# The last half chunk of an FFN, packed into two column tiles and zero-padded, with the value weights loaded between token blocks and a new task order

## The chip, the cores and the metric

The kernel runs on one core of a Trainium2 chip. The metric is device time in microseconds (us) of one execution. TensorE (PE) does matmuls, ScalarE (ACT) activations, VectorE (DVE) elementwise work and statistics, GpSimd (POOL) masks and small things, SyncE (SP) issues DMAs. A run lists its mean granted TensorE clock.

## The reference

One transformer layer on 2048 tokens, width 640, in bf16: layer norm, an attention with 32 heads of 20 in four segments of 512 tokens (causal softmax inside a segment, a running linear memory of the segments before), the output projection and a residual; then layer norm, an FFN of width 1728 with SiLU, and a residual.

```python
x = A_x
h = x + _A_ref(_layernorm(x, axis=-1), A_wq, A_wk, A_wv, A_wo, A_beta)
h2 = h + _B_ref(_layernorm(h, axis=-1), B_w1, B_w2)   # silu(x @ w1) @ w2
```

The point: 1728 = 13 x 128 + 64. Of the 14 chunks of the FFN's inner width the last is half a chunk, 64 rows.

## The kernel before

The program is a list of named tasks (`h1_2_13_0`: first FFN matmul, segment 2, chunk 13; `v00`: value projection, block 0; `qk..`: scores; `e..`: their exponentials; `pr..`: q and k projections; `fill39`: 39 dummy matmuls, "fillers", that keep PE busy where it would wait). A fixed string `ORDER` says in which order tasks are issued, on which engine and in which buffer. Each engine runs its own tasks strictly in that order. The parts that matter:

```python
for f in range(NF):                                   # 14 chunks
    fw = 128 if f < NF - 1 else FF - 128 * (NF - 1)   # the last: 64
    ...
    fns = [lambda e, c=c: e.matmul(bank(ps)[0:fw, lo:hi], lhsT=w1_sb[:, c, 128 * f:128 * f + fw],
                                   rhs=hT[:, c, lo:hi], start=(c == 0), stop=(c == NC - 1)) for c in range(NC)]
    # then th = tanh(0.5 * ps) on ACT, sT = (th + 1) * ps on DVE, both on fw partitions
...
for f in range(f0, f1):                               # h2, per token block i
    fw = 128 if f < NF - 1 else FF - 128 * (NF - 1)
    for hh in range(2):
        e.matmul(bank(ps, hh)[:, 0:320], lhsT=sT[0:fw, f, 128 * i:128 * i + 128],
                 rhs=w2_sb[0:fw, f, 320 * hh:320 * hh + 320], start=(f == 0), stop=(f == NF - 1))
```

At the start the four x blocks are loaded on SP's queue. wq, wk, wv follow on ACT's queue, after a warm-up activation. `SPLIT0 = (0, 1)` cuts the projections of the first two chunks into token halves, so that they can start on blocks 0 and 1.

The softmax here doesn't subtract the row's maximum and nothing guards it: scores larger than these inputs give would overflow.

## Time and profile before

| | before |
|---|---|
| time, median of 3 | 315.74 us |
| span in the profile | 313.7 us |
| PE busy | 301.0 us (96%) |
| tile configuration changes on PE, from the matmul records | 244 |

The page's table of busy time and the clock row of its 40 slices, kernel before:

```profile
span 313.7 us, 7314 instructions
...
PE 301.0 (96%) x2918; PEld 168.7 (54%) x2918; DVE 219.0 (70%) x495; ACT 227.3 (72%) x320; POOL 142.6 (45%) x280
...
PEclk9999799999999999999999999999999999999999
```

PE is busy nearly always, so one has to ask what it is busy with. The fifth slice of the clock row (31 to 39 us) shows a 7: there the granted clock was half for 3.4 us.

The stretch view of the kernel before (columns: stretch, its length, busy us of each engine with instruction counts, granted clock, DMA share, GB/s):

```profile
0.00:18.00 18.00, 15.55 (x131) 11.98 (x131) 11.76 (x40) 7.75 (x16) 6.24 (x28) 1.00 0.76 231
18.00:60.00 42.00, 39.33 (x449) 20.37 (x441) 30.79 (x86) 37.10 (x55) 21.92 (x47) 0.96 0.61 147
60.00:100.00 40.00, 38.56 (x439) 23.05 (x432) 30.81 (x79) 37.40 (x57) 24.48 (x53) 1.00 0.47 90
...
262.00:314.00 52.00, 48.01 (x300) 27.89 (x298) 24.14 (x42) 7.96 (x14) 3.13 (x8) 1.00 0.19 50
```

The fourth busy column is ACT: 37 of 42 and 37 of 40 us early on, 8 of 52 at the end. So PE and ACT together set the pace during the attention, and PE alone at the end.

Groups by shape, kernel before (count, busy us, mean ns of one):

```profile
L1162 PE MATMUL ps_all<-w_sb,sT 64*128 64x320 bf16 x32 | 7.1, 301 | 0.0
L1130 PE MATMUL ps_all<-hT,w_sb 128*64 128x512 bf16 x15 | 3.8, 384 | 0.0
L1144 DVE SCALAR_TENSOR_TENSOR sT<-th,ps_all 64x512 bf16<-64x512 f32 x3 | 2.0, 671 | 0.0
L1138 ACT ACTIVATE th<-ps_all 64x512 f32<-64x512 f32 x3 | 1.8, 587 | 0.3 <-DVE sT L1144 0.3
```

The half chunk on 64 partitions takes as long as a whole one on 128 (the whole ones take 679 and 608 ns on DVE and ACT). And there is a cost that no mean shows. The timeline of the kernel before, inside the last h2 matmuls:

```profile
303.13 0.11 PEld L1162 LDWEIGHTS ps_all<-w_sb,sT 64*128 64x128 bf16 x2 [0.26 <-issue]
303.50 1.47 PEld L1162 LDWEIGHTS ps_all<-w_sb,sT 128*128 128x128 bf16 x12 [0.26 <-issue]
```

The weight loader, which otherwise runs ahead during the matmuls, stands still for 0.26 us before and after the 64-row weights. The starts of the single matmuls in the trace say what that costs:

```
128-row to 128-row   136 ns from start to start
128-row to  64-row   231 ns
 64-row to  64-row   146 ns
 64-row to 128-row   228 ns
```

Elsewhere in the same trace matmuls of 512 columns start 216 ns apart: 192 columns more take 80 ns, so PE streams 2.4 columns per ns, and 320 columns are 133 ns. So the visit of two matmuls costs about 0.2 us more than two more full-height matmuls would, and there are 16 visits. The Trainium skill says, in "TensorEngine Tiling (Array Packing)", section Key Properties, that changing the tiling mode drains TensorE. The trace agrees and gives the price of this change: about 95 ns on the way in and 92 on the way out, and about 10 ns on the matmul after the first.

The first loads and the first score exponentials, kernel before: the page's DMA issues (KB each, us from issue to landing), then the timeline.

```profile
sT<-in_A_wq_dram ACTq DMA_DIRECT2D x1, 800.0 KB, 7.0
sT<-in_A_wk_dram ACTq DMA_DIRECT2D x1, 800.0 KB, 8.8
wv_sb<-in_A_wv_dram ACTq DMA_DIRECT2D x1, 800.0 KB, 10.2
```
```profile
18.25 1.51 ACT L888 ACTIVATE PTE<-ps_all 128x768 bf16<-128x768 f32 x2 [0.23 <-PE ps_all L877]
```

In the trace they land at 10.1, 12.4 and 14.4 us.

### The profile page before, as it was taken

What the parts mean: (1) busy time and instruction counts of PE and PEld (TensorE: products, weight loads), DVE (VectorE), ACT (ScalarE), POOL (GpSimd) and SP (SyncE); (2) the same over time, 40 slices, a digit from 0 to 9 for tenths busy, and PEclk for the clock granted to TensorE, in tenths of its full rate; (3) what the DMA queues carried; (4) which work ended last, traced back from release to release, by engine and by line L of the source; (5) the groups of instructions that cost most, each with busy time, mean ns of one, the idle gap of its engine ahead of it and who ended that gap; (6) DMA issues with size and microseconds to landing.
All of it is one profiled execution on the core that took longest, in us unless ns stands there. A gap on an engine that the chain in (4) does not pass through costs nothing.

```text
span 313.7 us, 7314 instructions
## 1 busy us (share of the span) xinstructions
PE 301.0 (96%) x2918; PEld 168.7 (54%) x2918; DVE 219.0 (70%) x495; ACT 227.3 (72%) x320; POOL 142.6 (45%) x280
## 2 busy tenths in 40 slices
PE   8899799999999999999999999999999999999995
PEld 6655454447555445575544544546554466744563
DVE  4888567787678876785979967569865594844622
ACT  3399798999989999988899898795889940004500
POOL 5227736344497465644748454536566540300000
PEclk9999799999999999999999999999999999999999
DMA  6884546951165300045442400223440006220002
GB/s 180 273 284 103 98 110 216 168 112 28 36 99 88 76 17 3 3 82 125 81 127 19 82 4 0 44 42 72 94 101 1 2 0 107 42 65 21 0 24 104
DMA packets 48353, 24.56 MB, mean 78 GB/s; under 512 B 38848, under 2 KB 47232, under 8 KB 48320
## 3 DMA queue, kind: packets, MB, share of 16 engines
q1 hardware_dynamic: 46352, 21.65, 31.4%
q10 hardware_dynamic: 1968, 2.46, 2.5%
q8 instruction: 23, 0.38, 0.5%
q14 instruction: 10, 0.08, 0.1%
HBM read 10.33 MB, written 2.62 MB: 41 GB/s over the span
## 4 chain that ended last, share of the span: by engine, by line
PE 69%; ACT 19%; DVE 5%; issue 2%; POOL 2%; DMA 1%; ACTq 0%; DVEq 0%
PE ps_all L1162 17%; PE ps_all L1130 13%; PE ps_all L805 11%; PE ps_all L1106 7%; PE ps_all L877 6%; PE ps_all L771 5%; ACT PTA L888 5%; PE ps_all L923 5%; ACT PTB L888 4%; ACT PTE L888 4%; ACT th L1138 3%; PE ps_all L597 2%; DVE on L989 2%; PE ps_all L952 1%; DMA oT<-otok 1%
## 5 line engine op out<-in xcount | busy, mean ns | idle before, releaser
L888 ACT ACTIVATE PTA<-ps_all 128x1024 bf16<-128x1024 f32 x64 | 62.5, 1025 | 7.4 <-PE ps_all L877 6.8
L1162 PE MATMUL ps_all<-w_sb,sT 128*128 128x320 bf16 (+1 forms) x448 | 67.7, 300 | 0.0
L1130 PE MATMUL ps_all<-hT,w_sb 128*128 128x512 bf16 (+3 forms) x350 | 67.1, 337 | 0.6 <-issue 0.5
L888 ACT ACTIVATE PTB<-ps_all 128x1024 bf16<-128x1024 f32 (+1 forms) x64 | 58.8, 969 | 7.8 <-PE ps_all L877 6.9
L900 POOL TENSOR_SCALAR_AFFINE_SELECT PTB<-PTB 128x512 bf16<-128x512 bf16 x64 | 41.3, 645 | 47.4 <-ACT PTB L888 45.1
L1138 ACT ACTIVATE th<-ps_all 128x512 f32<-128x512 f32 (+3 forms) x70 | 34.6, 519 | 34.8 <-PE ps_all L1130 30.4
L1144 DVE SCALAR_TENSOR_TENSOR sT<-th,ps_all 128x512 bf16<-128x512 f32 (+3 forms) x70 | 38.7, 574 | 20.7 <-ACT th L1138 20.3
L1162 PEld LDWEIGHTS ps_all<-w_sb,sT 128*128 128x128 bf16 (+1 forms) x448 | 40.5, 97 | 22.4 <-issue 7.9
L1130 PEld LDWEIGHTS ps_all<-hT,w_sb 128*128 128x128 bf16 (+1 forms) x350 | 32.0, 99 | 28.4 <-issue 4.8
L888 ACT ACTIVATE PTE<-ps_all 128x1024 bf16<-128x1024 f32 (+1 forms) x40 | 35.6, 937 | 4.2 <-PE ps_all L877 4.0
L900 POOL TENSOR_SCALAR_AFFINE_SELECT PTE<-PTE 128x512 bf16<-128x512 bf16 x40 | 25.8, 646 | 14.7 <-ACT PTE L888 13.3
L703 DVE BATCH_NORM_STATS2 stt<-x_tok 128x6 f32<-128x320 bf16 x64 | 28.0, 479 | 2.8 <-DMA x_tok<-in_A_x_dram 2.5
L771 PE MATMUL ps_all<-wv_sb,xT 128*128 128x320 bf16 x160 | 25.8, 311 | 1.3 <-ACT PTE L888 1.3
L805 PE MATMUL ps_all<-xT,wqr 128*128 128x512 bf16 (+1 forms) x110 | 24.9, 360 | 1.6 <-DVE wqr L677 1.3
L997 POOL TENSOR_TENSOR otok<-on 128x320 bf16<-128x320 bf16 x24 | 19.1, 800 | 14.6 <-DVE on L989 14.6
L814 DVE CAST QK<-ps_all 128x512 bf16<-128x512 f32 (+1 forms) x34 | 21.0, 628 | 6.4 <-PE ps_all L805 5.7
L1172 DVE SCALAR_TENSOR_TENSOR x_tok<-ps_all,x_tok 128x640 bf16<-128x640 f32 x16 | 12.9, 819 | 17.2 <-PE ps_all L1162 17.2
L805 PE MATMUL ps_all<-xT,wkr 128*128 128x512 bf16 (+1 forms) x110 | 24.8, 361 | 0.0
L1106 PE MATMUL ps_all<-wo_sb,oT 128*128 128x320 bf16 x160 | 23.8, 299 | 0.7 <-DMA oT<-otok 0.5
L712 POOL TENSOR_TENSOR rst<-mvt,eps_c 128x1 f32<-128x1 f32 x32 | 6.9, 216 | 35.2 <-DVE mvt L706 32.3
L877 PE MATMUL ps_all<-QK 20*128 20x256 bf16 (+3 forms) x360 | 20.7, 288 | 1.5 <-ACT PTA L888 0.6
L771 PEld LDWEIGHTS ps_all<-wv_sb,xT 128*128 128x128 bf16 x160 | 15.2, 101 | 9.7 <-DMA xT<-xn_rot 1.5
(77 smaller groups left out, 409.9 us busy)
## 6 DMA issues: line engine op xcount, KB each, us to landing
out_dram<-x_tok SPq DMA_DIRECT2D x16, 160.0 KB, 2.0
w_sb<-in_B_w_dram SPq DMA_DIRECT2D x5, 432.0 KB, 6.3
x_tok<-in_A_x_dram SPq DMA_DIRECT2D x3, 640.0 KB, 5.8
w_sb<-in_B_w_dram SPq DMA_DIRECT2D x3, 480.0 KB, 4.2
QKV<-QK SPq DMA_DIRECT2D x16, 72.0 KB
sT<-in_A_wq_dram ACTq DMA_DIRECT2D x1, 800.0 KB, 7.0
sT<-in_A_wk_dram ACTq DMA_DIRECT2D x1, 800.0 KB, 8.8
wv_sb<-in_A_wv_dram ACTq DMA_DIRECT2D x1, 800.0 KB, 10.2
```

The costliest lines, as they stand in the source:

```text
L703: T.add(DV, lambda e, hh=hh: e.bn_stats(out=stt[:, s, 6 * hh:6 * hh + 6], in_=xb[:, 320 * hh:320 * hh + 320]), reads=R((xa, xsub)), writes ...
L771: fns.append(lambda e, c=c, hh=hh: e.matmul(bank(ps, hh)[:, 0:320], lhsT=xT[:, c, 128 * i:128 * i + 128], rhs=wv_sb[:, c, 320 * hh:320 * h ...
L805: fns = [lambda e, kc=kc: e.matmul(bank(ps)[:, lo:hi], lhsT=wt[:, kc, c, :], rhs=xT[:, kc, lo:hi], start=(kc == 0), stop=(kc == NC - 1)) f ...
L814: (lambda e: e.tensor_copy(out=o, in_=i_))
L877: fns.append(lambda e, j=j, o=o, r=r, q0=q0, q1=q1, qa=qa, ka=ka: e.matmul(ps_all[:, o:o + q1 - q0], lhsT=ka[32 * r:32 * r + DH, 128 * j:1 ...
L888: T.add(AC, lambda e: e.activation(out=pt[:, pta.slot, q0:q0 + 2, 0:width], in_=sc3[:, b0:b0 + 2, 0:width], func=ACT.Exp, scale=SCALE), re ...
L900: fns.append(lambda e, v=v: e.affine_select(out=v, in_=v, pattern=[[0, 4], [1, 128]], compare_op=ALU.is_ge, fill=0.0, base=0, channel_mult ...
L1106: fns.append(lambda e, c=c, hh=hh: e.matmul(bank(ps, hh)[:, 0:320], lhsT=oT[:, c, 128 * i:128 * i + 128], rhs=wo_sb[:, c, 320 * hh:320 * h ...
L1130: fns = [lambda e, c=c: e.matmul(bank(ps)[0:fw, lo:hi], lhsT=w1_sb[:, c, 128 * f:128 * f + fw], rhs=hT[:, c, lo:hi], start=(c == 0), stop= ...
L1138: T.add(AC, lambda e: e.activation(out=th[0:fw, tha.slot, lo:hi], in_=bank(ps)[0:fw, lo:hi], func=ACT.Tanh, scale=0.5), reads=R((ps, [0])) ...
L1144: T.add(DV, lambda e: e.scalar_tensor_tensor(out=sT[0:fw, f, lo:hi], in0=th[0:fw, tha.slot, lo:hi], scalar=1.0, in1=bank(ps)[0:fw, lo:hi], ...
L1162: fns.append(lambda e, f=f, fw=fw, hh=hh: e.matmul(bank(ps, hh)[:, 0:320], lhsT=sT[0:fw, f, 128 * i:128 * i + 128], rhs=w2_sb[0:fw, f, 320 ...
```

## The change

Four things at once:

1. h1 of the half chunk becomes two column tiles: the even token blocks go to output partitions 0 to 63, the odd ones to 64 to 127, side by side. Tanh and multiply then run on 128 partitions and half as many columns.
2. h2 reads that packed tile at full height. Its weights exist twice, once with rows 64 to 127 zero (even blocks), once with rows 0 to 63 zero (odd blocks). The zeros come from the warm-up activation, which is now a tanh of 0.
3. All first loads are in SP's queue, in the order x0, x1, wv, x2, x3, beta, wq, wk, without waiting for the warm-up. The value matmuls of blocks 0 and 1 come first in PE's order.
4. `SPLIT0` is empty, and the whole `ORDER` is new, with 41 fillers instead of 64.

```diff
-SPLIT0 = (0, 1)
+SPLIT0 = ()
 ORDER = """   # (all lines replaced)
-zpad:0 x0:0 x1:1 x2:2 warm x3:3 ... w_q:0 w_k beta ... w_wv:0 n1_ap0:0 fill39:0 n1_tp0:0 ...
+zpad:0 x0:0 x1:1 w_wv:0 x2:2 x3:3 beta w_q:0 w_k ... fill21:0 n1_tp0:0 ... n1_te1/A v00:0 v01:2 ...
-    for b in range(4):
-        load_x(b, 1, -100 + b, (2.2, 3.0, 3.7, 4.2)[b], "fix", (SP,))
+    load_x(0, 1, -100, 2.30, "fix", (SP,))
+    load_x(1, 1, -99, 2.33, "fix", (SP,))
+    load_w("wv", wv_sb[:, :, :], cw(A_wv), -98, 4.96, [(W["wv"], [0])], "fix", (SP,))
     ...
+    tail = f == NF - 1
+    if tail:
+        hv = hT[:, :, :].rearrange("p c (i h t) -> p c h i t", h=2, t=128)
+        fns = [lambda e, c=c, k=k: e.matmul(
+            bank(ps)[64 * k:64 * k + 64, lo:hi], lhsT=w1_sb[:, c, 128 * f:FF],
+            rhs=hv[:, c, k, b0 // 2:b1 // 2, :], start=(c == 0), stop=(c == NC - 1),
+            tile_position=(0, 64 * k)) for c in range(NC) for k in range(2)]
     ...
-    fw = 128 if f < NF - 1 else FF - 128 * (NF - 1)
+    t0, fr = (128 * i, f) if f < NF - 1 else (128 * (i // 2), f + i % 2)
     for hh in range(2):
-        ... lhsT=sT[0:fw, f, 128 * i:128 * i + 128], rhs=w2_sb[0:fw, f, 320 * hh:320 * hh + 320] ...
+        ... lhsT=sT[:, f, t0:t0 + 128], rhs=w2_sb[:, fr, 320 * hh:320 * hh + 320] ...
```

## The prediction

> **What bounds the kernel now.** The page's table of busy time has TensorE (PE) busy 301.0 of 313.7 us. By the starts of single matmuls in the trace, streaming is 261 us, 6.8 of it filler matmuls; 244 changes of tile configuration at about 0.095 us are 23 us; some 25 us are stalls, more than half before 60 us. In the stretch view ScalarE is the second limit: busy 37.1 of 42 us between 18 and 60 us, 37.4 of 40 to 100, and only 8.0 of 52 after 262 us, where PE alone sets the pace.
>
> **What the change removes and adds.**
>
> 1. Half chunk in h2. Equal matmuls start 136 ns apart; into the 64-row weights it is 231 ns, then 146, and out again 228. So each of 16 visits costs about 0.2 us. The Trainium skill ("TensorEngine Tiling (Array Packing)", Key Properties) says that changing the mode drains TensorE; the trace agrees. Zero-padded to 128 rows the matmul takes the same 133 ns and no switch. Counted in the two orders, changes fall from 244 to 217: 27 x 0.095 = 2.6 us, plus 0.3 for slower first ones.
>
> 2. Half chunk in h1. Today 5 matmuls of 512 columns at 216 ns per segment (segment 0: twice 256). As two column tiles, 5 pairs of 256 columns at about 112 ns: the packed value matmuls (L923) already start 2 to 5 ns apart, as the skill's "TensorE: Matmul & The Clock Gate", Part 3, says. 4 x 0.52 = 2.1 us of PE. Tanh and multiply on the half chunk go from 587 and 671 ns to about 390 and 417 in three segments, and from two pairs to one in segment 0: about 1 us each on ScalarE and VectorE.
>
> 3. Start. wq, wk, wv land at 10.1, 12.4, 14.4 us; ScalarE's warm-up holds their issue until 3.15 us, and between 4.4 and 6 us DMA moves about 130 KB per us against 370 later. With one queue I estimate wv at 6, wq at 9, wk at 11.3 us. Two blocks' value matmuls then replace fillers (64 become 41), and the first score exponential starts at about 15.5 us instead of 18.25. Gain 1.5 to 2.7 us for PE and ScalarE alike.
>
> 4. Unsplit projections save a few evictions. The task order is all new: about 2 us either way, unknown.
>
> **On the critical path.** After 262 us all PE savings count: two segments' h2 (1.7) and one h1 (0.5), 2.2 us. Before, ScalarE and PE alternate: the start's gain plus part of the other 2.8 us of PE, 3 to 5 us. Together about 6.3 us: 315.7 becomes 309.4 us, range 306.0 to 312.8. On the 2% line: faster 0.5, within 2% 0.48, slower 0.02.
>
> **What would show it.** h2 matmuls evenly 136 ns apart through each block; about 217 changes; half-chunk h1 pairs 2 to 5 ns apart, a group about 0.6 us; wv landed near 6 us, first score exponential near 15.5 us; the last stretch (last segment's h1 to last h2 matmul) shorter by about 1.3 us.
>
> **What would make it wrong.** wk landing later than 12.4 us (the start then gains nothing); the column tiles' weight loads (109 ns each) not hiding behind 107 ns of streaming; a longer clock drop (today half clock from 36 to 39 us) with fewer fillers; or the new order adding stalls between 20 and 160 us that eat the savings.

## More of the kernel before

In the first 18 us ACT has done only 7.75 us of work.

## The result, and the profile after

| | before | after |
|---|---|---|
| median of the same rounds | 315.62 us (4 runs) | 306.18 us (4 runs) |
| ratio | | 0.9711, 95% interval 0.9678 to 0.9744 |
| the same, second measurement | 314.82 us (11 runs) | 305.99 us (6 runs), 0.9725 (0.9698 to 0.9752) |
| span in the profile | 313.7 us | 303.9 us |
| configuration changes on PE | 244 | 217 |

A ratio is the mean time of one kernel's fast runs over the mean of the other's fast runs of the same rounds, so it is not quite the ratio of the medians. The change is faster by 2.8 to 2.9%, some 9 us; 6.3 us were predicted, and the time lies near the lower end of the range.

The same lines of the page after:

```profile
span 303.9 us, 7238 instructions
...
PE 290.1 (95%) x2876; PEld 165.8 (55%) x2900; DVE 219.1 (72%) x489; ACT 226.8 (75%) x322; POOL 143.9 (47%) x280
...
PEclk9999999999999999999999999999999999999999
```

PE is busy 10.9 us less, ACT and DVE as long as before, and the half-clock stretch is gone. Some records of matmuls are missing after (2876 matmuls beside 2900 weight loads), so sums over matmuls are short by up to a per cent, while starts and spans are not.

The stretch view after:

```profile
0.00:18.00 18.00, 15.15 (x99) 8.97 (x101) 11.48 (x34) 10.20 (x20) 6.04 (x25) 1.00 0.65 208
18.00:60.00 42.00, 38.79 (x475) 19.70 (x477) 35.63 (x98) 38.83 (x56) 24.71 (x50) 1.00 0.70 173
60.00:100.00 40.00, 39.16 (x456) 23.72 (x456) 31.85 (x77) 38.40 (x57) 24.75 (x57) 1.00 0.36 77
```

By 18 us ACT has done 10.20 us instead of 7.75, and it stays busier until 100 us. PE's busy time in the first stretch is a little lower, but fewer of its matmuls are fillers: useful streaming by 18 us, added up from the columns of each record, is 8.2 us instead of 6.8.

Groups by shape after, the answer to the four lines of before:

```profile
L1176 PE MATMUL ps_all<-w_sb,sT 128*128 128x320 bf16 x448 | 65.2, 299 | 0.0
L1138 PE MATMUL ps_all<-hT,w_sb 128*64 128x256 bf16 x30 | 2.2, 277 | 0.0
L1158 DVE SCALAR_TENSOR_TENSOR sT<-th,ps_all 128x256 bf16<-128x256 f32 x29 | 11.7, 416 | 9.1 <-ACT th L1152 8.8
L1152 ACT ACTIVATE th<-ps_all 128x256 f32<-128x256 f32 x29 | 10.8, 391 | 5.0 <-PE ps_all L1138 4.6
```

There are no 64-row matmuls any more, and the half chunk's tanh and multiply take 391 and 416 ns (three of the 29 in each group are half chunks; segment 0 has two more, of 128 columns, at 282 and 284 ns). The timeline of one packed h1 group after:

```profile
288.51 0.47 PEld L1138 LDWEIGHTS ps_all<-hT,w_sb 128*64 128x64 bf16 x10 [0.26 <-issue]
288.52 0.74 PE L1138 MATMUL ps_all<-hT,w_sb 128*64 128x256 bf16 x10
```

Single starts inside this group are 3, 130, 3, 106, 4, 105, 4, 106, 3 ns apart: the two tiles of a pair start together, and a pair follows a pair after 109 ns, about the 107 ns that 256 columns take. Five of the old 512-column matmuls were 216 ns apart. The weight loads, of 109 ns in the mean, hide. That is what the Trainium skill says of packed tiles ("TensorE: Matmul & The Clock Gate", Part 3: about 4 ns from one tile to the next).

The loads after (page, DMA issues) and the first score exponentials (timeline):

```profile
wv_sb<-in_A_wv_dram SPq DMA_DIRECT2D x1, 800.0 KB, 5.6
sT<-in_A_wq_dram SPq DMA_DIRECT2D x1, 800.0 KB, 7.8
sT<-in_A_wk_dram SPq DMA_DIRECT2D x1, 800.0 KB, 9.6
```
```profile
17.12 1.50 ACT L891 ACTIVATE PTE<-ps_all 128x768 bf16<-128x768 f32 x2
```

In the trace wv, wq, wk land at 7.4, 11.6 and 13.8 us (6.8, 11.0, 13.2 in a second profile). wk, which gates the first scores, comes later than before, not earlier. The first exponential still starts 1.1 us earlier (1.7 in the second profile). One profile's first exponential is a weak measure, though: e1 and e2 below, which keep the old start, have it at 17.6 and 17.1 us. By the 17th the two orders are well apart: 38.7 to 40.3 us in five profiles of the old order and start, 33.5 to 35.0 in six of the new (before, e1, e2, e6, e8; after, e3, e4, e5, e9, e11).

### The profile page after: what moved, and what is told of

Its sections match the earlier page's. It is cut to its first block, busy times and chain, and to the rows that moved or that the text cites. A ratio compares the mean times of both kernels' runs of the same rounds, so it can differ in the third digit from the quotient of the medians.

```text
span 303.9 us, 7238 instructions
## 1 busy us (share of the span) xinstructions
PE 290.1 (95%) x2876; PEld 165.8 (55%) x2900; DVE 219.1 (72%) x489; ACT 226.8 (75%) x322; POOL 143.9 (47%) x280
## 4 chain that ended last, share of the span: by engine, by line
PE 72%; ACT 12%; DVE 7%; DMA 4%; issue 2%; POOL 1%; SPq 1%; DVEq 0%; ACTq 0%
PE ps_all L1176 18%; PE ps_all L1143 16%; PE ps_all L808 12%; PE ps_all L1109 7%; PE ps_all L880 6%; PE ps_all L926 5%; ACT PTA L891 4%; ACT PTB L891 3%; DMA sT<-in_A_wq_dram 3%; PE ps_all L774 2%; PE ps_all L955 2%; ACT PTE L891 2%; PE ps_all L959 1%; DMA oT<-otok 1%; PE ps_all L1048 1%
## 5 line engine op out<-in xcount | busy, mean ns | idle before, releaser
L1176 PE MATMUL ps_all<-w_sb,sT 128*128 128x320 bf16 x448 | 65.2, 299 | 0.0
L1143 PE MATMUL ps_all<-hT,w_sb 128*128 128x512 bf16 (+1 forms) x315 | 60.1, 335 | 0.9 <-issue 0.5
L1152 ACT ACTIVATE th<-ps_all 128x512 f32<-128x512 f32 (+2 forms) x70 | 34.0, 507 | 35.3 <-PE ps_all L1143 26.8
L1158 DVE SCALAR_TENSOR_TENSOR sT<-th,ps_all 128x512 bf16<-128x512 f32 (+2 forms) x70 | 38.0, 561 | 27.0 <-ACT th L1152 25.8
L1176 PEld LDWEIGHTS ps_all<-w_sb,sT 128*128 128x128 bf16 x448 | 42.3, 98 | 19.3 <-issue 2.1
L1143 PEld LDWEIGHTS ps_all<-hT,w_sb 128*128 128x128 bf16 x325 | 30.3, 98 | 23.9 <-issue 1.3
L808 PE MATMUL ps_all<-xT,wqr 128*128 128x512 bf16 x92 | 23.4, 380 | 1.9 <-ACT xT L741 1.1
L1000 POOL TENSOR_TENSOR otok<-on 128x320 bf16<-128x320 bf16 x24 | 19.0, 793 | 11.3 <-DVE on L992 11.3
L808 PE MATMUL ps_all<-xT,wkr 128*128 128x512 bf16 x94 | 23.4, 380 | 0.5 <-issue 0.3
L903 POOL TENSOR_SCALAR_AFFINE_SELECT PTA<-PTA 128x512 bf16<-128x512 bf16 x24 | 15.5, 647 | 16.5 <-ACT PTA L891 16.4
L1186 DVE SCALAR_TENSOR_TENSOR x_tok<-ps_all,x_tok 128x640 bf16<-128x640 f32 x16 | 13.0, 818 | 13.8 <-PE ps_all L1176 13.8
L992 DVE TENSOR_TENSOR on<-ps_all,rd 128x640 bf16<-128x640 f32 x24 | 19.8, 825 | 0.8
```

The source lines that it names most:

```text
L808: fns = [lambda e, kc=kc: e.matmul(bank(ps)[:, lo:hi], lhsT=wt[:, kc, c, :], rhs=xT[:, kc, lo:hi], start=(kc == 0), stop=(kc == NC - 1)) f ...
L903: fns.append(lambda e, v=v: e.affine_select(out=v, in_=v, pattern=[[0, 4], [1, 128]], compare_op=ALU.is_ge, fill=0.0, base=0, channel_mult ...
L992: T.add(DV, lambda e: e.tensor_tensor(out=on[:, ona.slot, :, :].rearrange("p b (x e) -> p b x e", e=DH), in0=v[:, :, :, 0:DH], in1=r2.unsq ...
L1143: fns = [lambda e, c=c: e.matmul(bank(ps)[:, lo:hi], lhsT=w1_sb[:, c, 128 * f:128 * f + 128], rhs=hT[:, c, lo:hi], start=(c == 0), stop=(c ...
L1152: T.add(AC, lambda e: e.activation(out=th[:, tha.slot, lo:hi], in_=bank(ps)[:, lo:hi], func=ACT.Tanh, scale=0.5), reads=R((ps, [0])), writ ...
L1158: T.add(DV, lambda e: e.scalar_tensor_tensor(out=sT[:, f, lo:hi], in0=th[:, tha.slot, lo:hi], scalar=1.0, in1=bank(ps)[:, lo:hi], op0=ALU. ...
```

## The experiments

The theory at this point: the FFN part pays its PE time, in full where PE sets the pace; the start and the new order pay the rest. Rivals: the FFN part makes everything; or it is hidden and the order makes everything. For the start: early wv itself; one queue instead of two; or the clock.

All ratios are to the kernel before in the same rounds. There were four sets of rounds, on four chips: e1 to e4; e5, e6, e7, e9; e8, e10, e11; and e12. A difference in us between kernels of different sets is a little less sure.

| run | what it is | median us | ratio (95%) |
|---|---|---|---|
| e1 | before + both FFN parts | 309.64 | 0.9855 (0.9815 to 0.9895) |
| e2 | before + zero-padded h2 only | 312.83 | 0.9941 (0.9908 to 0.9975) |
| e3 | after, old FFN tail | 311.92 | 0.9916 (0.9889 to 0.9943) |
| e4 | after, h2 on 64 rows | 309.51 | 0.9841 (0.9812 to 0.9871) |
| e5 | after, h1 unpacked | 309.07 | 0.9828 (0.9801 to 0.9855) |
| e6 | before, one load queue | 314.53 | 0.9991 (0.9962 to 1.002) |
| e7 | after, wv last | 309.09 | 0.9806 (0.9767 to 0.9845) |
| e8 | before, more filler at 31.7 us | 313.71 | 0.9976 (0.9947 to 1.0004) |
| e9 | after, again | 305.99 | 0.9725 (0.9698 to 0.9752) |
| e10 | e7 + 26 fillers | 310.19 | 0.9868 (0.9833 to 0.9902) |
| e11 | after, wv behind all x | 306.83 | 0.976 (0.9724 to 0.9796) |
| e12 | before, new start only | 317.8 | 1.0106 (1.008 to 1.0132) |

### e1: both FFN parts in the old order

```diff
 # before, with h1 tail, h2 tail and doubled w2 rows of the changed kernel; zeros from VectorE
+for o in (w2_sb[64:128, NF - 1, :], w2_sb[0:64, NF, :]): e.memset(o, 0.0)
-... w_w2_4/S ...
+... w_w2_4/S w_w2_5/S ...
```

> The kernel before with its own task order and start, but with both halves of the FFN change (h1 half chunk as two column tiles, h2 with zero-padded weights). Theory A (the FFN part is worth its PE time wherever PE sets the pace, and the order is worth the rest): PE saves 2.1 us of streaming, 27 configuration changes (2.6 us) and 0.3 us, of which all 2.2 us after 262 us and about half of the rest count: 312.0 us, between 311 and 313. Rival B (the FFN part alone makes nearly the whole gain of 9.5 us): 307 to 308 us. Rival C (in the old order the savings are eaten by waits for ScalarE): 314 us or more. Configuration changes in the trace: 217.

Measured: 309.64 us, 1.45% or 4.6 us less, with 217 changes. That lies between theory A's range (311 to 313) and rival B's (307 to 308). The PE saving (2.1 us of streaming, 2.6 of changes, 0.3 of slow first matmuls: 5.0 us) counts nearly in full, in an order that was not made for it. The runs with the full clock say the same: four of e1, mean 309.2 us, against four of the kernel before, 314.1.

### e2: the zero-padded h2 alone, in the old order

```diff
-fw = 128 if f < NF - 1 else FF - 128 * (NF - 1)     # in h2 only
+fw = 128                                            # rows 64 to 127 of both operands zeroed once
```

> The kernel before with only the zero-padded h2: h1 as before. Theory A: 16 visits to 64-row weights cost 0.2 us each; 1.7 us of it after 262 us counts in full, the rest in part: 313.3 us (312.5 to 314.0). In the stretch after 262 us the h2 matmuls start 136 ns apart throughout, and that stretch is 1.7 us shorter. Rival (the drain is hidden by other waits): 315.5 us.

Measured: 0.9941, 1.9 us less, inside theory A's range. The last stretch, from the last segment's first h1 matmul to the last h2 matmul, is the cleanest place to read it, as PE never waits there. From the starts in the traces:

```
                        length of the last stretch   changes in it
before                        31.15 us                     9
e2  h2 padded                 30.41                        2
e5  after, h1 unpacked        30.41                        2
e4  after, h2 on 64 rows      30.62                        9
after, e1, e9                 29.88                        2
```

Some records are missing here too. In all of these traces but that of the kernel before, the first h1 matmul of the stretch has none: there are two matmuls fewer than weight loads, one lost inside (a step of 432 ns) and one at the edge. Its start is put one step before the first that is recorded (216 ns; 226 behind 64-row weights). Without that the stretch would seem 0.2 us shorter than it is. In e10 and e11, where no record is missing, it is 29.88 us as well.

Seven changes fewer are worth 0.74 us here, from before to e2 and from e4 to after alike. The packing of h1 is worth 0.53 us, as costed. (The 1.7 us in the expectation was the sum over two segments, wrongly put on this one.)

### e3 and e4: the new order and start without the FFN parts, or without the padded h2 only

```diff
 # e3: h1 and h2 tails of the kernel before, all else as after
 # e4: h1 as after; h2 of the half chunk as a row tile on 64 rows
-lhsT=sT[:, f, t0:t0 + 128], rhs=w2_sb[:, fr, ...]
+lhsT=sT[r0:r1, f, t0:t0 + 128], rhs=w2_sb[r0:r1, fr, ...], tile_position=(r0, 0)   # r0 = 64 * (i % 2)
```

> The changed kernel with the FFN tail put back as it was (h1 half chunk over 512 columns on 64 rows, h2 on 64 rows), so only the new order and the new start are left. Theory A (FFN part worth 3.5 to 5 us on the new order): 306.2 + 4.3 = 310.5 us (309.7 to 311.3). Rival B (the FFN part makes nearly all): 314 to 316 us. Rival C (the FFN part is hidden): 306 to 307 us. First 40 us as in the changed kernel: the 17th pair-exponential of the scores at 34 us, not 40.

> The changed kernel with h1 as column tiles but h2 reading the half chunk on 64 rows (rows 0 to 63 or 64 to 127) as a row tile. Only the drains come back: 26 more configuration changes, 16 visits at about 0.2 us, 3.2 us of PE. Theory A: 306.2 + 2.8 = 309.0 us (308.2 to 309.6). Rival (drains hidden): under 307 us.

Measured: e3 0.9916, 311.92 us, above theory A's range (309.7 to 311.3) and below rival B's; the 17th exponential came at 35.0 us. So order and start alone are worth 0.84%, 2.6 us, and the FFN parts on top of them 1.9 to 2.0%, some 6 us. In the old order the FFN parts were worth 4.6 us (e1). The parts add up to 2.3%, the whole is 2.8 to 2.9%. That the two help each other by the half a per cent between is not shown: the intervals of e1, e3 and e9, taken together, are as wide as that.

e4's median is 309.51 us, inside theory A's range. It has two kinds of runs: three with a mean clock of 0.994 (310.46, 309.83, 310.21 us) and three with 1.0 (308.92, 308.34, 309.19; mean 308.82). Against the 305.98 us mean of e9 (other rounds), whose six runs all had the full clock, the latter give 2.8 us for the drains, the number that was expected. The rest of e4's excess is a half-clock stretch, from 35.9 to 39.3 us in its profile. Up to there e4 issues the same tasks as the changed kernel (its first h2 matmul starts at 82.6 us). So the changed kernel is not safe from that drop; its ten listed runs did not have it. The line just before, of the changed kernel and then of e4 (timeline):

```profile
34.21 1.53 PE L774 MATMUL ps_all<-wv_sb,xT 128*128 128x320 bf16 x10 [0.39 <-DMA xT<-xn_rot]
```
```profile
35.37 2.38 PE L774 MATMUL ps_all<-wv_sb,xT 128*128 128x320 bf16 x10 [1.10 <-DMA xT<-xn_rot]
```

In e4 PE waits 1.10 us for a DMA, and the clock halves about half a microsecond after the wait.

### e5 and e9: h1 unpacked, and the changed kernel in the same rounds

```diff
 # e5: h1 tail of the kernel before (64 rows, 512 columns), h2 still 128 rows with zeros
```

> The changed kernel with the h1 half chunk unpacked again (5 matmuls of 512 columns into 64 rows, tanh and multiply over 512 columns), h2 still zero-padded. Theory A: it gives back 2.1 us of PE streaming, nearly all on the path: 2.0 to 2.8 us more than the changed kernel of the same rounds. Rival (most of the packing's worth is the shorter tanh and multiply, or it is hidden): less than 1 us more.

> The changed kernel itself, once more, so that the other kernels of this call are compared with it in the same rounds: ratio 0.971 to the kernel before (0.968 to 0.975), 305.5 to 306.5 us. The first score exponential starts near 17.1 us; a drop of the granted clock near 36 us may or may not come.

Measured: 0.9828 against 0.9725, 3.2 us between the means, more than the 2.0 to 2.8 expected, though the spread of the twelve runs leaves 2.4 to 4.1. 0.53 us of it are in the last stretch (table above). The last score exponential starts at 244.1 us instead of 241.2, of which 0.6 us are there at the first one already (by as much the two profiles of the changed kernel differ there). PE's part up to there is 1.6 us (three segments); the half chunk's tanh and multiply, 0.2 us and more longer each time, are the likely rest, but no run separates them.

### e6: one load queue in the kernel before

```diff
-load_w("q", ..., "fix", (AC,))      # and k, wv; waiting for the warm-up
+load_w("q", ..., "fix", (SP,))      # behind x0..x3, no wait; beta behind wv
```

> The kernel before with wq, wk and wv behind the four x blocks in the one load queue and not waiting for the warm-up; wv stays last, the task order is otherwise kept. Theory S1 (one queue without the wait brings wk about 0.7 to 1.5 us earlier, and what follows moves with it): wq near 9.3, wk near 11.5, wv near 13.8 us; 0.7 to 1.5 us faster than the kernel before. Rival S2 (the start is not what sets the pace; the order of tasks in the first 40 us is): within 0.4 us of the kernel before.

Measured: 0.9991, the same, as rival S2 had it. wq, wk and wv landed at 10.5, 12.8 and 14.9 us, no earlier than with two queues and a wait. The Trainium skill says that DMAs from different engines run on the same 16 DMA engines ("DMA: Bandwidth & Descriptors", section Issuing engines are not separate DMA queues), and this run agrees: the queue is not what was gained. The edit also moved the small beta load from before wq to behind wv; that brought no earlier landing either (last section).

### e7 and e10: wv last, without and with fillers in its place

```diff
-zpad:0 x0:0 x1:1 w_wv:0 x2:2 x3:3 beta w_q:0 w_k ... n1_te1/A v00:0 v01:2 n1_st2:2 ...
+zpad:0 x0:0 x1:1 x2:2 x3:3 beta w_q:0 w_k w_wv:0 ... n1_te1/A n1_st2:2 ...           # e7
+                                                 ... n1_te1/A fill26:0 n1_st2:2 ...  # e10
 # both: v00 behind the first score matmuls, v01 two projections later
```

> The changed kernel with wv last in the load queue instead of between the token blocks, and the value matmuls of blocks 0 and 1 moved behind the first score matmuls. Theory S3 (wv early only delays wk, which gates the first scores): wk near 11.5 us instead of 13.8, first score exponential near 15 us instead of 17.1, total 1 to 2 us less than the changed kernel of the same rounds. Rival S4 (wv early is what makes the start good, as it fills PE while wq and wk come): 0.5 to 2 us more.

> The kernel with wv last (309.1 us, with a half-clock stretch at 12 us in 4 of 6 runs; 306.8 and 307.4 in the two without) plus 26 filler matmuls where the changed kernel has the value matmuls of blocks 0 and 1, so that TensorE is as busy there but does nothing useful. Theory K (early wv helps in two ways: it keeps the clock up, about 2 us, and takes two value matmuls out of the later stretch, about 1 us): no half clock before 20 us in any run, 307.0 us (306.5 to 307.6). Rival L (it is all the clock): 306.0 us as the changed kernel. Rival M (it is all the useful work): 308.5 us or more.

Measured: e7 is 2.7 us slower than the changed kernel of the same rounds (mean 308.67 against 305.98), although wk landed earlier (12.8 us). S3 falls. (wk was expected at 11.5 us, the total at 1 to 2 us less.) Four of its six runs had a mean clock below 0.995; in the profile it is half from 12.1 to 15.5 us. The two others took 306.77 and 307.37 us, 1.1 us more than e9 in the mean. PE in e7 just before and in that stretch (timeline):

```profile
9.40 0.45 PE L732 MATMUL ps_all<-ident,xn_rot 128*128 128x128 bf16 x5 [1.97 <-DVE xn_rot L723]
9.70 0.60 PE L599 MATMUL ps_all<-zpad 128*128 128x256 bf16 x4
10.73 0.45 PE L732 MATMUL ps_all<-ident,xn_rot 128*128 128x128 bf16 x5 [0.44 <-DVE xn_rot L723]
12.48 1.91 PE L808 MATMUL ps_all<-xT,wqr 128*128 128x512 bf16 x4 [1.29 <-ACT xT L741]
14.18 2.97 PE L808 MATMUL ps_all<-xT,wkr 128*128 128x512 bf16 x10
```

Fifteen projection matmuls, which take 3.2 us at full clock (216 ns each), run into the half clock. In the changed kernel the 20 value matmuls stand where e7 has the hole of 1.97 us.

So e10 fills the hole with fillers. Five of its six runs have the full clock at 0.999 or more, and the first exponential starts at 16.1 us, half a microsecond earlier than in e9. Yet it takes 310.19 us, the number of rival M. So keeping the clock up with fillers does not replace early wv. The timeline of e10 shows where part of the time goes:

```profile
17.18 1.24 PE L808 MATMUL ps_all<-xT,wqr 128*128 128x512 bf16 x5
18.26 1.53 PE L774 MATMUL ps_all<-wv_sb,xT 128*128 128x320 bf16 x10
19.63 1.24 PE L808 MATMUL ps_all<-xT,wkr 128*128 128x512 bf16 x5
20.80 0.34 PE L880 MATMUL ps_all<-QK 20*128 20x256 bf16 x8
```
```profile
17.52 0.64 ACT L823 ACTIVATE ex<-QK 128x512 bf16<-128x512 bf16 x1
20.91 0.60 ACT L816 ACTIVATE QK<-ps_all 128x512 bf16<-128x512 f32 x1 [2.75 <-PE ps_all L808]
```

The value matmuls, done late, stand between the projections that ACT needs next, and ACT idles for 2.75 us in the middle of its crowded stretch. The third score exponential, in e9 and then in e10 (timeline):

```profile
19.09 1.51 ACT L891 ACTIVATE PTE<-ps_all 128x768 bf16<-128x768 f32 x2
```
```profile
21.40 1.51 ACT L891 ACTIVATE PTE<-ps_all 128x768 bf16<-128x768 f32 x2
```

That is 2.3 us, and e7's profile has the same idle 2.75 us at this place. Most of what is left of the 4.4 us between the means of e10 and e9 (other rounds) arises far from the start: in e10's profile PE stands still for 1.10 us before 158.3 us and for 0.89 us before 257.9 us, the second time for a DMA, and e7's and e9's profiles have neither wait. So the late value matmuls cost about 2.3 us by the traces, but 1.1 us by e7's two runs with the full clock, and the order around them is made by hand. How the worth of early wv splits between useful work and clock is not settled.

### e11: wv ahead of wq and wk, but behind all x blocks

```diff
-zpad:0 x0:0 x1:1 w_wv:0 x2:2 x3:3 beta
+zpad:0 x0:0 x1:1 x2:2 x3:3 w_wv:0 beta
```

> The changed kernel with wv behind all four x blocks but still ahead of wq and wk: x2 and x3 land near 5 us instead of 7.5, wv near 7.5 instead of 7, wk unchanged near 13.5. Theory N (wk gates the first scores, so the place between the blocks is worth nothing beside a place before wq and wk): within 0.5 us of the changed kernel, 305.5 to 306.7 us. Rival O (between the blocks is what matters): 1 us or more slower.

Measured: 306.83 us, 0.976; between theory N and rival O. Its mean is 1.0 us above that of e9 (0.6 without its one half-clock run), though in other rounds, and the intervals overlap. In the profile wv landed at 8.9 us and wk at 14.5 us; the latter is 0.7 and 1.3 us later than in the two profiles of the changed kernel. wv's issue moves from 1.73 to 2.67 us, as each issue takes SP about 0.45 us. The place between the blocks may be worth something, at most about 1 us; these runs do not show it.

### e8: fillers against the clock drop in the kernel before

```diff
-... e0ya0 fill6:3 qk4x0:0 ...
+... e0ya0 fill14:3 qk4x0:0 ...
```

> The kernel before with 14 instead of 6 filler matmuls at 31.7 us, ahead of the place where the granted clock halves (36 to 39 us) in 16 of its 22 listed runs. The listed runs without that drop are 0.8 us faster in the mean. Theory P (the drop costs 0.8 us and follows from idle TensorE before it): the drop is gone or rarer and the kernel is 0.3 to 0.8 us faster. Rival Q (the drop has another cause or costs nothing): drop as often as before, time within 0.3 us or longer by the added filler.

Measured: 0.9976; none of its six runs has the drop, four of eleven runs of the kernel before in the same rounds do. Over the four sets of rounds the kernel before lists 44 runs: 26 with a mean clock of 0.995 or less (mean 315.0 us) and 18 with 0.999 or more (mean 314.2 us). So the drop costs about 0.8 us where it comes. As it comes in some 60% of the runs, about 0.5 us of the gain of the changed kernel are the clock. That fits theory P, but less firmly than it looks: at four in eleven, six runs without the drop would come by chance one time in fifteen, and the interval of the time just reaches 1.

### e12: the new start in the old order

```diff
-zpad:0 x0:0 x1:1 x2:2 warm x3:3 ... w_q:0 w_k beta ...        fill39:0 n1_tp0:0 ... fill10:2 n1_tp1:0 ... fill9:2 pr000x:0
+zpad:0 x0:0 x1:1 w_wv:0 x2:2 warm x3:3 ... beta w_q:0 w_k ... fill21:0 n1_tp0:0 ... fill6:2 n1_tp1:0 n1_te1/A v00:2 ve00/A:0 v01:6
+n1_ap2:0 n1_ap3:1 ve01/D n1_tp2:4 n1_te2/A n1_tp3:6 n1_te3/D ... re_wq0/D:0 re_wq1/D pr000x:0
```

> The kernel before, FFN and task order as they were, with only the new start: one load queue, wv behind x1, and the value matmuls of blocks 0 and 1 done at once in place of fillers (27 fillers instead of 58 before the first projections). Theory R (early wv pays by itself, since 2.7 us of value matmuls leave the crowded stretch from 15 to 26 us): wv near 7 us, wk near 13.5 us, 1.0 to 2.5 us faster than the kernel before. Rival T (early wv pays only with the new task order): within 0.5 us of the kernel before, or slower because wk comes 1 us later.

Measured: 1.0106, about 3 us slower. Rival T. wk landed at 14.9 us, and the first exponential started at 23.2 us instead of 18.2. PE and ACT of e12 (timeline):

```profile
13.82 0.45 PE L730 MATMUL ps_all<-ident,xn_rot 128*128 128x128 bf16 x5 [1.78 <-DVE Vx L783]
15.52 1.34 PE L806 MATMUL ps_all<-xT,wqr 128*128 128x256 bf16 x10 [1.24 <-DVE wqr L678]
...
22.79 0.34 PE L878 MATMUL ps_all<-QK 20*128 20x256 bf16 x8
```
```profile
20.66 0.87 ACT L814 ACTIVATE QK<-ps_all 128x512 bf16<-128x512 f32 x2 [4.82 <-PE ps_all L806]
```

After the value matmuls PE waits twice for DVE. DVE is late itself: x2 and x3, now behind wv in the queue, landed at 9.0 and 9.4 us (4.6 and 5.1 before), and DVE gets to the copies of wq, which landed at 12.7 us, only at 15.1. The clock halves from 16.6 to 20.0 us in this profile (all six runs list 0.995 or less), and ACT idles for 4.82 us. What the run shows is that early wv was no gain in this order; which order it needs was tried only with the changed kernel's.

## Why the prediction was right, and where it was not

The time, 306.2 us, is just inside the range of 306.0 to 312.8 (306.0 in the second measurement), and the class was put at even chances. 6.3 us were forecast and some 9 came. Point by point:

**h2 padded: right.** 217 changes were counted ahead and are there, the h2 matmuls are 136 ns apart throughout, and the last stretch shrank by 1.27 us (1.3 predicted). Undone alone (e4, full-clock runs against e9 in other rounds) it costs 2.8 us, of the 2.9 us costed.

**h1 packed: mechanism right, size low.** The pairs start 3 ns apart and 109 ns from pair to pair. 2.1 us of PE were costed; undoing it costs 3.2 us (e5; 2.4 to 4.1 by the spread). One detail was wrong: segment 0 still has two half chunks, of half the columns. Tanh and multiply save 0.8 and 1.0 us over all segments, about the 1 us each that was forecast.

**"Part of the other 2.8 us of PE" counts before 262 us: mis-sized.** The term was 2.2 us plus a part, so 2.2 to 5.0 us for the FFN. The FFN parts alone are worth 4.6 us in the old order (e1) and some 6 us in the new one (e3 against the changed kernel). Where PE and ACT are both nearly always busy and wait for each other, a saving on PE was not lost while ACT was the next limit. That it exceeds PE's 5.0 us in the new order is within the noise of e3 and e9 (4.8 to 7.2 us); it may also come from ACT's and DVE's own savings or from an order made for these durations. The runs don't separate these.

**The start: the step failed, and that it gained all the same was luck.** wk was estimated at 11.3 us and landed at 13.2 to 13.8; the first exponential was predicted at 15.5 us and came at 16.6 to 17.1. By the prediction's own words, "wk landing later than 12.4 us (the start then gains nothing)", nothing should have been left. Yet ACT had done 9.3 to 10.8 us of work by 18 us in five profiles with the new order and start (after, e3, e4, e5, e9), and 7.6 to 8.6 in the five with the old ones: about 2 us more, the 1.5 to 2.7 predicted. Early wv is not the reason for that part, as e10, with wv last, has 10.6. What early wv brings shows behind it: the third exponential, 2.3 us earlier than in e10. How much of the 2.6 us of order and start (e3) is the start's own, no run shows. The one-queue step of the argument was empty: e6 gains nothing. The estimate took the peak of 370 KB per us for the whole load; the trace after shows dips to 125 and to 62 KB per us in half-microsecond slices.

**The order: unknown, said to be 2 us either way.** Order and start together are 2.6 us without the FFN parts (e3), and the start alone in the old order loses about 3 us (e12). In these runs the start paid only with the new order. What the new order is worth with the old start was not run.

**The clock: the warning pointed the wrong way.** Fewer fillers were feared to lengthen the half-clock stretch. The changed kernel has none in ten listed runs; that is about 0.5 us of the gain. Why it has none is not shown, and in part it is luck: e4, with the same tasks up to the place, has the drop in three of six runs.

## What to carry to other kernels

Look for changes of tile configuration inside a dense run of matmuls: they hide in no mean, only in the starts from one matmul to the next, and an odd half chunk can be padded with zeros to full height at the same streaming time. If the half chunk's outputs can sit side by side in two column tiles, the engines that read them gain as well. A load moved earlier paid here only with an order that put its work into an idle time, so move the order with it. Before a stretch is measured from record to record, count the records, as a lost one at its edge changes its length. And check the granted clock of every run before believing a difference of less than a per cent.

## What the Trainium skill lacked or had wrong

- "TensorEngine Tiling (Array Packing)", Key Properties: it says that a mode change drains TensorE but gives no price. Here a change between 128 and 64 rows costs about 95 ns each way and 10 ns on the next matmul (136 ns become 231, 146 and 228), and 64-row weights in a 128-row run cost 0.2 us per visit. Zero-padding to 128 rows, not mentioned, took 133 ns of streaming per 320 columns, as much as 64 rows do.
- "TensorE: Matmul & The Clock Gate", HAM oscillation (HAM is the page's name for the block that gates the clock): its rule is "no PE-idle gaps >~3.4µs". Here the clock halved for 3.4 us after far shorter gaps: in the kernel before the longest gap just ahead of it was 1.26 us, with PE busy 1.78 of the 3.42 us before; in e7 it was 1.97 us, with 1.34 of 3.41 us busy; in e4 1.10 us, with 1.89 of 3.41. The page's next section, on a second failure mode, does name frequent short idle times as a cause, but without a length. The kernel before had the drop in 26 of 44 runs. That it varies from run to run agrees with the page's free-running window (Part 1).
- "DMA: Bandwidth & Descriptors", section Bandwidth, gives rates by size for one transfer; it has nothing on what a small broadcast load does to the large ones around it in the queue. In both profiles the rate of the first loads dips while the 8 KB beta load (128 packets of 64 bytes) is under way: to 71 KB per us at 4.5 us before, to 62 at 7.5 us after, against 370 elsewhere. But e6, which has beta behind wv, is a test of it: its beta packets run from 11.1 to 14.4 us, the rate between 2 and 11 us is never under 182, and still wq and wk land no earlier (10.5 and 12.8 us). And after has a dip to 125 at 3.5 us, before any beta packet. So beta fits as the cause of the deep dip, but moving it was no gain in e6, which changed the queue at the same time; alone it was not tested.
